# Weights signed by a parametric relu on ScalarE, keys' halves in buffers of their own, and batches prepared in ten timed steps

## The chip, the cores and the metric

One core of one Trainium2 chip. The time is the device time of one execution in microseconds (us), as the median of several runs. The engines are TensorE (PE, matrix products), VectorE (DVE), ScalarE (ACT), GpSimd (POOL) and SyncE (SP), whose queue issues most of the DMA transfers. Each engine works through its own queue in order.

## The reference

```python
k_p = k.reshape(B, H, Sp, 8, D).mean(axis=3)      # B=8, H=8, S=576, D=64, Sp=72
v_p = v.reshape(B, H, Sp, 8, D).mean(axis=3)
scores = q @ k_p.T / 8; scores -= max(scores)
attn = exp(scores); attn /= sum(attn) + 1e-9
x = (attn @ v_p), as 4608 tokens x 512
h = x @ moe_w_in                                  # 512 x 2048
g = where(h >= 1, h, where(h <= -1, 0, (h + 1)**2 / 4))
x = g @ moe_w_out                                 # 2048 x 512
h = x @ moe2_w_in; g = h / (1 + exp(-h))          # the same sizes
out = g @ moe2_w_out
```

## The kernel before

**Numbers.** The products run in float16. Each operand is scaled by a power of two and kept as two halves, hi and lo, and each product is three: hi by hi, hi by lo, lo by hi. The four weights arrive as float64, read as pairs of 32-bit words. A piece of weights (128 x 1024 values, `raw`, or a tile that is lent as a room for it) is turned into halves in this chain: ACT takes the absolute value of the high words, scaled down (`Abs`, L185 or L247); DVE takes their maximum with an accumulator (L190 or L248); PE and DVE spread that maximum over the partitions (L107, L108) and a power of two follows from it in two tiny steps (`w_scale`); DVE shifts the float's bits (L93), ORs the sign bit in from the high word (L202 or L267) and the rest of the mantissa from the low word (L208 or L270); ACT scales (L215 or L273) and casts to hi (L220 or L275); POOL subtracts to get lo (L221 or L276). `moe_w_in` comes in nine pieces, `moe_w_out` in four quarters of two pieces. The second MLP's weights are loaded twice, first only for their maximum (L111), then for the conversion.

**First MLP.** Nine tiles of 512 tokens. For a tile there are 16 steps; each makes one chunk of 128 hidden units in 12 products of 128x512 (tile `hps`, weights `wa`), and the chunk three steps older goes into the output `y` with 12 products (weights `wb`). Between the two, ACT (L823, L830, L862) and DVE (L93, L834, L863) work out the piecewise activation `g`. In the first tile the weights are still being converted, and its `y` products stand behind all its `hps` products, quarter by quarter of `moe_w_out`. The second MLP starts at about 960 us and is 18 half-tiles.

**Attention.** It is worked out ahead of the first MLP, a query tile of 128 rows in four slots: `att_qT` (mean of absolute values on ACT, L465; hi and lo on ACT and DVE, L367 and L368; a DMA transpose from SP, L554), `att_scores` (PE, L564), `att_norm`, then a transpose of the attention weights (`aT`, from SP, L622) and the product with the values (`att_pv`, PE, L657). In the first eight steps of the second tile there are two slots to a step, later one.

**Batches.** Each of the eight batches needs its pooled keys and values. Half of the raw rows are loaded by SP (`kv_load`), the other half added by POOL's accumulating DMA (`kv_more`), DVE adds what is left (L459, L462), ACT takes the mean (L465), PE and DVE turn it into a scale, ACT and DVE split hi and lo, ACT copies both (L499), and SP issues two DMA transposes into `kT` (L502). All this for a batch is called at the first slot of the first query tile that needs it (`batches`). The keys' hi and lo are two tiles `rows`, from the same pool of two buffers as each query tile's own `rows`: the mean of the next query tile (L465) writes into a buffer from which a key transpose reads.

**Order.** A scheduler, led by an estimate of times, puts the instructions of each engine in order; `tc.issue_after` holds single ones behind others. On the chip each engine keeps that order.

Of the kernel before, what the change touches and what calls it, by code (L numbers as in the profile page):

```python
# [28 lines left out]
FLOOR_DOWN = _bits((1023 - 60 - 8 * 112) << 20)  # L29
# [3 lines left out]
def tile_pooled_attention_two_mlps(  # L33
# [79 lines left out]
    cols, free = const.tile([128, 80], F32, name="cols"), iter(range(80))  # L113
# [60 lines left out]
    def steps(piece, dst, scale, loaded, mx=None, seen=None, fill=None):  # L174

        t = {}

        def s0():
            r = t["r"] = piece()
            x = xfp.tile([128, XF], F32, tag="xf", name="xf")
            t["x"] = x[:, 0:r.shape[1] * r.shape[2] // 2].rearrange("p (a b) -> p a b", a=r.shape[1])
            nc.scalar.activation(out=t["x"], in_=high(r, F32), func=AF.Abs, scale=DOWN)  # L185

        def s1():
            x, m = t["x"], mx()
            with after_lows():
                nc.vector.tensor_scalar(  # L190
                    out=x, in0=x, scalar1=0.0, scalar2=FLOOR_DOWN, op0=ALU.max, op1=ALU.max, accum_out=m
                )
            seen()

        def s2():
            xi = t["x"].bitcast(I32)
            with after_lows():
                ts(xi, xi, 3, op0=ALU.logical_shift_left)

        def s3():  # L200
            xi = t["x"].bitcast(I32)
# [4 lines left out]
        def s4():  # L206
            xi = t["x"].bitcast(I32)
            lows.append(nc.vector.scalar_tensor_tensor(  # L208
                out=xi, in0=low(t["r"]), scalar=29, in1=xi, op0=ALU.logical_shift_right, op1=ALU.bitwise_or
            ))  # L210
            loaded()

        def s5():
            x, s = t["x"], scale()
            nc.scalar.activation(out=x, in_=x, func=AF.Copy, scale=s)  # L215
# [9 lines left out]
        return [s0] + [s1] * bool(mx) + [s2, s3, s4, s5]  # L225

    def new_scale(e, g):
        s = sm.tile([128, 1], F32, tag="ws", name="ws", bufs=3)
        w_scale(e, s, g)
        return s  # L230

    def weight_in(w, e, tiles, cuts, rooms):
# [4 lines left out]
        mx, s, g = col(n), col(n), col(n)  # L237
# [4 lines left out]
        def room32(p):  # L242
            return tiles[p].rearrange("p a c f -> p (a c f)").bitcast(F32).rearrange("p (a b) -> p a b", a=KD)

        def look(p):
            x = room32(p)
            nc.scalar.activation(out=x, in_=high(held[p], F32), func=AF.Abs, scale=DOWN)  # L247
            nc.vector.tensor_scalar(  # L248
                out=x, in0=x, scalar1=0.0, scalar2=FLOOR_DOWN, op0=ALU.max, op1=ALU.max, accum_out=mx[:, p:p + 1]
            )  # L250

        def scales(a, b):
# [6 lines left out]
            w_scale(e[:, a:b], s[:, a:b], g[:, a:b])  # L259

        def work(p):
# [3 lines left out]
            xi = x.bitcast(I32)  # L265
            ts(xi, room32(p).bitcast(I32), 3, op0=ALU.logical_shift_left)
            nc.vector.scalar_tensor_tensor(  # L267
                out=xi, in0=high(r, I32), scalar=-0x80000000, in1=xi, op0=ALU.bitwise_and, op1=ALU.bitwise_or
            )
            nc.vector.scalar_tensor_tensor(  # L270
                out=xi, in0=low(r), scalar=29, in1=xi, op0=ALU.logical_shift_right, op1=ALU.bitwise_or
            )
# [1048 lines left out]
```

## Time and profile before

| what | value |
|---|---|
| time, median of 3 runs | 1641.39 us (1640.28 to 1647.74) |
| the profiled execution: time, span | 1640.59 us, 1638.8 us |
| mean granted clock of TensorE | 0.969 of 2.4 GHz |
| busy PE | 1534.5 us (94%) |
| busy DVE | 1208.5 us (74%) |
| busy ACT | 894.1 us (55%) |
| busy POOL | 581.8 us (36%) |

The span is the part of the execution that the profiler records; about 1.8 us lie around it. The first tile of the first MLP ends at 209 us with its output `y`, the second at 333 us, and from there most tiles take 86 to 98 us. PE is busy nearly throughout from 440 us on; the idle time lies before that. The rows below are cited by group.

### The profile page before, as it was taken

The numbers are of one execution on the slowest core, as the hardware profiler recorded it, in microseconds if no ns is written. First come the engines' busy times: TensorE is split into PE (matmuls) and PEld (weight loads), VectorE is DVE, ScalarE is ACT, GpSimd is POOL, SyncE is SP. The second block draws the span as 40 slices with busy tenths as digits, with TensorE's granted clock in tenths as the row PEclk, the third lists the DMA queues.
The fourth block names the chain that finished last, engine by engine and source line by source line (L and its number), as shares of the span: only waits on it lengthen the run. The fifth ranks groups of instructions, "written<-read, shape, count | busy, mean of one in ns | idle before, by whom it ended". The sixth has DMA issues, their size and how long they took to land.

```text
span 1638.8 us, 34439 instructions
## 1 busy us (share of the span) xinstructions
PE 1534.5 (94%) x14278; PEld 1052.6 (64%) x14278; DVE 1208.5 (74%) x2166; ACT 894.1 (55%) x1418; POOL 581.8 (36%) x507
## 2 busy tenths in 40 slices
PE   6765889799999999999999999999999999999998
PEld 5322434344444444444444479999999999999998
DVE  6898868566777687787767767777776777777765
ACT  4477455455666556574566555554444544455543
POOL 2342513113343332331355424433333433343322
PEclk9876899899999999999999999999999999999999
DMA  9573688927547366255574330001100000000000
GB/s 295 123 181 86 122 165 190 186 73 130 145 107 166 89 111 138 81 140 163 194 302 145 148 129 28 27 27 32 36 27 28 27 34 34 27 27 28 27 15 27
DMA packets 226157, 166.35 MB, mean 102 GB/s; under 512 B 154960, under 2 KB 193616, under 8 KB 226000
## 3 DMA queue, kind: packets, MB, share of 16 engines
q1 hardware_dynamic: 216592, 155.88, 35.4%
q0 software_dynamic: 9408, 8.27, 3.7%
q8 instruction: 112, 1.84, 0.5%
q14 instruction: 45, 0.37, 0.1%
HBM read 102.76 MB, written 33.55 MB: 83 GB/s over the span
## 4 chain that ended last, share of the span: by engine, by line
PE 50%; DVE 16%; DMA 9%; issue 9%; ACT 9%; POOL 6%; SPq 1%; DVEq 0%; POOLq 0%; ACTq 0%
PE y L120 5%; PE y L122 5%; PE y L121 5%; PE hps L120 4%; PE hps L122 4%; PE hps L121 4%; PE y L1024 4%; PE y L1025 4%; PE y L1026 4%; PE hb L122 4%; PE hb L121 4%; PE hb L120 4%; POOL c L724 4%; DMA kT<-rows 3%; DMA yin<-y 2%
## 5 line engine op out<-in xcount | busy, mean ns | idle before, releaser
L121 PE MATMUL hb<-xl,wc 128*128 128x128 f16 x2016 | 347.6, 219 | 0.0
L122 PE MATMUL hb<-xh,wc 128*128 128x128 f16 x2016 | 347.6, 219 | 0.0
L120 PE MATMUL hb<-xh,wc 128*128 128x128 f16 x2016 | 347.6, 219 | 0.0
L368 DVE SCALAR_TENSOR_TENSOR g<-c,tsg,g 128x512 f16<-128x512 f32 x252 | 228.7, 910 | 97.8 <-ACT g L367 97.8
L1024 PE MATMUL y<-wd,g 128*128 128x256 f16 x1008 | 274.7, 273 | 1.9 <-DVE ob L1037 1.8
L1026 PE MATMUL y<-wd,g 128*128 128x256 f16 x1008 | 274.7, 273 | 0.0
L1025 PE MATMUL y<-wd,g 128*128 128x256 f16 x1008 | 274.7, 273 | 0.0
L120 PE MATMUL hps<-xh,wa 128*128 128x512 f16 x576 | 222.7, 387 | 36.2 <-ACT wa L275 19.7
L964 ACT ACTIVATE c<-c,tc 128x512 f32<-128x512 f32 x144 | 103.2, 717 | 230.8 <-DVE c L961 230.8
L367 ACT ACTIVATE g<-c,tsg 128x512 f16<-128x512 f32 x252 | 177.6, 718 | 85.8 <-POOL c L727 48.3
L122 PE MATMUL hps<-xh,wa 128*128 128x512 f16 x576 | 220.7, 384 | 3.8 <-POOL wa L276 3.8
L121 PE MATMUL hps<-xl,wa 128*128 128x512 f16 x576 | 222.8, 387 | 0.4 <-DVE xl L368 0.2
L120 PE MATMUL y<-g,wb 128*128 128x512 f16 x544 | 210.0, 388 | 11.6 <-ACT wb L220 9.8
L122 PE MATMUL y<-g,wb 128*128 128x512 f16 x544 | 210.6, 387 | 4.7 <-POOL wb L221 4.7
L121 PE MATMUL y<-g,wb 128*128 128x512 f16 x544 | 210.7, 387 | 0.5 <-DVE g L863 0.5
L121 PEld LDWEIGHTS <-wc 128*128 128x128 f16 x2016 | 197.3, 98 | 2.4
L120 PEld LDWEIGHTS <-wc 128*128 128x128 f16 x2016 | 197.3, 98 | 2.2
L122 PEld LDWEIGHTS <-wc 128*128 128x128 f16 x2016 | 197.3, 98 | 0.0
L961 DVE TENSOR_TENSOR c<-c,hb 128x512 f32<-128x512 f32 x252 | 167.8, 681 | 38.6 <-PE hb L122 36.2
L834 DVE SCALAR_TENSOR_TENSOR g<-g,tbr,u 128x512 f32<-128x512 f32 x144 | 126.4, 878 | 59.0 <-ACT u L830 58.1
L724 POOL TENSOR_TENSOR c<-c 128x512 f32<-128x512 f32 x108 | 164.0, 1533 | 2.8
L603 POOL TENSOR_TENSOR e<-e,den 128x576 f32<-128x576 f32 x36 | 49.6, 1378 | 313.6 <-DVE den L602 226.2
(185 smaller groups left out, 2710.3 us busy)
## 6 DMA issues: line engine op xcount, KB each, us to landing
raw<-in_moe_w_out_dram SPq DMA_DIRECT2D x21, 1024.0 KB
raw<-in_moe_w_in_dram SPq DMA_DIRECT2D x18, 1024.0 KB
y<-y SPq DMA_DIRECT2D x36, 256.0 KB
yin<-y SPq DMA_DIRECT2D x18, 512.0 KB
out_dram<-ob SPq DMA_DIRECT2D x36, 256.0 KB
d<-hl SPq DMA_DIRECT2D x32, 256.0 KB
qt<-in_q_dram SPq DMA_DIRECT2D x31, 256.0 KB
wc<-d SPq DMA_DIRECT2D x8, 896.0 KB
```

What stands on the lines that cost most here:

```text
L120: nc.tensor.matmul(out=acc, lhsT=wh, rhs=xh, start=start, stop=False)
L121: nc.tensor.matmul(out=acc, lhsT=wh, rhs=xl, start=False, stop=False)
L122: anchor["pe"] = nc.tensor.matmul(out=acc, lhsT=wl, rhs=xh, start=False, stop=stop)
L367: a = nc.scalar.activation(out=hi, in_=x, func=AF.Copy, scale=s)
L368: return a, nc.vector.scalar_tensor_tensor(out=lo, in0=x, scalar=s, in1=hi, op0=ALU.mult, op1=ALU.subtract)
L724: nc.gpsimd.tensor_tensor(out=out, in0=a, in1=b, op=ALU.subtract)
L834: anchor["dve"] = nc.vector.scalar_tensor_tensor(out=g32_t[s], in0=g32_t[s], scalar=r["br"], in1=u_t.pop(s), op0=ALU.subtract, op1=ALU.max)
L961: nc.vector.tensor_tensor(out=out, in0=x, in1=y, op=ALU.add)
L964: nc.scalar.activation(out=x, in_=x, func=AF.Silu, scale=r["c1"])
L1024: nc.tensor.matmul(out=acc, lhsT=xh, rhs=wh, start=start, stop=False)
L1025: nc.tensor.matmul(out=acc, lhsT=xh, rhs=wl, start=False, stop=False)
L1026: nc.tensor.matmul(out=acc, lhsT=xl, rhs=wh, start=False, stop=stop)
```

## The change

1. The sign and the magnitude of a weight come from one ACT instruction, a parametric relu with a scale, a bias just under zero and a large negative slope (`signed`); DVE's sign OR is gone. The maximum is taken by DVE from the raw high words (`abs_max`, L113), so the scale is needed before the ACT instruction and not behind the low words. `w_scale` has six tiny steps instead of two.
2. The keys' halves have a tag of their own, `krows`, with two buffers.
3. From batch 2 on, a batch is prepared in ten steps, each at a fixed number of slots ahead of the first slot of its first query tile (`PREP`), and each held behind what was last issued on five engines. Sums have two buffers instead of three.
4. The six steps of the first quarter of `moe_w_out` are spread over steps 6 to 13 of the first tile instead of all at step 10, and the small scale tiles of a query or token tile are columns of one tile (`small`).

```diff
-    def w_scale(e, s, g, up=14):
-        ts(e.bitcast(I32), g.bitcast(I32), 0x7FF00000, 3, ALU.bitwise_and, ALU.logical_shift_left)
-        bits(s, e, -1.0, 254 + up)
+    def w_scale(e, d, s, g, up=14):
+        t = sm.tile([128, 8], F32, tag="wt", name="wt", bufs=2)
+        a, b = (t[:, 4 * i:4 * i + g.shape[1]] for i in range(2))
+        ts(a, g, FLOOR_HIGH, DOWN, ALU.max, ALU.mult)
+        ts(b.bitcast(I32), a.bitcast(I32), EXP_MASK, op0=ALU.bitwise_and)
+        bits(d, b, -1.0, 15 + TOP)
+        ts(b.bitcast(I32), a.bitcast(I32), 0x00700000, 3, ALU.bitwise_and, ALU.logical_shift_left)
+        bits(s, b, -1.0, 254 - 8 * TOP + up)
+        ts(e.bitcast(I32), a.bitcast(I32), 0x7FF00000, 3, ALU.bitwise_and, ALU.logical_shift_left)
+    def signed(x, r, d):
+        nc.scalar.activation(out=x, in_=high(r, F32), func=AF.Prelu, scale=d, bias=under, alpha=-LIFT)
...
     def steps(piece, dst, scale, loaded, fill=None):
         def s0():
-            nc.scalar.activation(out=t["x"], in_=high(r, F32), func=AF.Abs, scale=DOWN)
+            signed(t["x"], r, scale()[0])
         def s1():
-            x, m = t["x"], mx()
-            with after_lows():
-                nc.vector.tensor_scalar(
-                    out=x, in0=x, scalar1=0.0, scalar2=FLOOR_DOWN, op0=ALU.max, op1=ALU.max, accum_out=m
-                )
-            seen()
+            with after_lows():
+                shifted(t["x"])
         def s2():
+            lows.append(with_low(t["x"], t["r"]))
+            loaded()
         def s3():
-            nc.vector.scalar_tensor_tensor(
-                out=xi, in0=high(t["r"], I32), scalar=-0x80000000, in1=xi, op0=ALU.bitwise_and, op1=ALU.bitwise_or
-            )
...
     def weight_in(w, e, tiles, cuts, rooms):
         def look(p):
-            x = room32(p)
-            nc.scalar.activation(out=x, in_=high(held[p], F32), func=AF.Abs, scale=DOWN)
-            nc.vector.tensor_scalar(
-                out=x, in0=x, scalar1=0.0, scalar2=FLOOR_DOWN, op0=ALU.max, op1=ALU.max, accum_out=mx[:, p:p + 1]
-            )
+            abs_max(mx[:, p:p + 1], high(held[p], F32))
...
     def weight_out(w, e, dst, tiles):
+        def look(i):
+            abs_max(mx[d][:, half:half + 1], high(held[i], F32))
+        def search(d):
+            s[d] = new_scale(e[:, d:d + 1], all_of(m[:, 0:1]))
...
-            st[2 * d][:-1] + st[2 * d + 1][:-1] + [st[2 * d][-1], st[2 * d + 1][-1]] for d in range(KD)
+            [lambda d=d: look(2 * d), lambda d=d: look(2 * d + 1), lambda d=d: search(d), st[2 * d][:-1],
+             st[2 * d + 1][:-1], [st[2 * d][-1], st[2 * d + 1][-1]]] for d in range(KD)
...
+    def keys_mean(b):
+        krows[b] = [ap.tile([SPT, H, 2, D], F16, tag="krows", name="krows", bufs=2) for _ in range(2)]
+        sums_mean(sums[b, "k"], km, krows[b][0])
     def batch_keys(b):
-        x = sums.pop((b, "k"))
-        hi, lo = rows(SPT), rows(SPT)
-        s = sums_scale(x, km, ek[:, b:b + 1], hi)
-        split(hi[:, :, 0], lo[:, :, 0], x, s)
+        hi, lo = krows[b]
+        split(hi[:, :, 0], lo[:, :, 0], sums.pop((b, "k")), search(SPT, km, ek[:, b:b + 1]))
...
-    def batches(i):
-        b = segs(i)[-1][2]
-        if i > NI and segs(i - 1)[-1][2] != b:
-            pool_to(8 * b + 4)
-            batch_keys(b)
-            pool_to(8 * b + 8)
-            batch_values(b)
...
+    def due(b):
+        return 4 * (S * b // 128 - 2 * NI) - 3
+    PREP = [
+        (16, lambda b: kv_load(b, "k")), (15, lambda b: kv_load(b, "v")),
+        (13, lambda b: kv_more(b, "k")), (12, lambda b: kv_more(b, "v")),
+        (7, lambda b: sums_of(b, "k")), (6, lambda b: sums_of(b, "v")),
+        (5, lambda b: keys_mean(b)), (4, lambda b: values_mean(b)),
+        (3, lambda b: batch_keys(b)), (2, lambda b: batch_values(b)),
+    ]
+    def prepare(n):
+        for b in range(2, B):
+            for before, f in PREP:
+                if due(b) - before == n:
+                    with behind("pe", "act", "dve", "pool", "sp"):
+                        f(b)
...
+    W2S = [6,7,9,10,11,13]
...
-        if s == 10:
-            run(*work2[0])
+        if s in W2S:
+            with behind("dve", "act", "pe"):
+                w2step(0, W2S.index(s))
```

Three places in the engines' order follow. In the names, `xf` is a piece of weights in work, `wm` a maximum, `u`, `g` and `stash` belong to the activation, `sum`, `rows`, `krows` and `skv` to the keys and values.

DVE before, in the first tile, at the first two pieces of `moe_w_out`:

```order
L190 TENSOR_SCALAR xf,wm_879<-xf 128x1024
L462 TENSOR_TENSOR sum<-raw 72x512
L93 TENSOR_SCALAR u<-g_726,tlim 128x512
L863 TENSOR_TENSOR g_730<-g_693,g_730 128x512
L93 TENSOR_SCALAR xf<-xf 128x1024
L93 TENSOR_SCALAR u<-g_755,tlim 128x512
L202 SCALAR_TENSOR_TENSOR xf<-raw,xf 128x1024
L93 TENSOR_SCALAR xf<-wa_136 128x1024
L368 SCALAR_TENSOR_TENSOR rows<-sum,skv,rows 80x8x64
L834 SCALAR_TENSOR_TENSOR g_726<-g_726,tbr,u 128x512
L208 SCALAR_TENSOR_TENSOR xf<-raw,xf 128x1024
L190 TENSOR_SCALAR xf,wm_879<-xf 128x1024
```

DVE after, at the same two pieces:

```order
L95 TENSOR_SCALAR xf<-xf 128x1024
L191 SCALAR_TENSOR_TENSOR xf<-raw,xf 128x1024
L95 TENSOR_SCALAR xf<-xf 128x1024
L350 SCALAR_TENSOR_TENSOR v_115<-sum,skv,v_115 72x512
L191 SCALAR_TENSOR_TENSOR xf<-raw,xf 128x1024
L95 TENSOR_SCALAR xf<-xf 128x1024
L95 TENSOR_SCALAR u<-g_996,small 128x512
L859 TENSOR_TENSOR stash<-g_944,stash 128x512
L830 SCALAR_TENSOR_TENSOR g_969<-g_969,small,u 128x512
L191 SCALAR_TENSOR_TENSOR xf<-wb_128,xf 128x1024
L113 TENSOR_REDUCE wm_1126<-raw 128x1
```

The row of the sign (L202) has gone from between shift and low words. In the last row a maximum (L113) stands in DVE's queue whose piece is loaded into the buffer that the first low words of this piece of the queue (its second row) have just freed.

ACT before, at batch 3, in the second tile:

```order
L367 ACTIVATE rows<-sum,skv 80x8x64
L367 ACTIVATE v_115<-sum,skv 72x512
L499 COPY rows<-rows 80x8x64
L862 CAST g_2583<-g_2531 128x512
L499 COPY rows<-rows 80x8x64
L823 ACTIVATE g_2579<-hps,tbr,tc_1292 128x512
L830 ACTIVATE u<-u,trsg 128x512
L862 CAST g_2648<-g_2579 128x512
L583 ACTIVATE e<-e,cq 128x576
L465 ACTIVATE rows,eq<-qt 128x512
L823 ACTIVATE g_2644<-hps,tbr,tc_1292 128x512
L465 ACTIVATE rows,eq<-qt 128x512
```

ACT after, at the same batch:

```order
L349 ACTIVATE krows<-sum,skv 80x8x64
L448 ACTIVATE rows,eq<-qt 128x512
L487 COPY krows<-krows 80x8x64
L858 CAST g_2465<-g_2410 128x512
L598 CAST e_116<-e 128x4x72
L598 CAST e_117<-e 128x4x72
L487 COPY krows<-krows 80x8x64
L349 ACTIVATE v_115<-sum,skv 72x512
L819 ACTIVATE g_2461<-hps,small 128x512
L349 ACTIVATE rows<-qt,sq 128x8x64
L349 ACTIVATE xh<-att,small 128x4x128
```

Before, the two copies of the keys are followed by the means of two query tiles into `rows`; now a mean into `rows` stands between split and copies, and the keys are in `krows`.

SP before, at the key transposes of batch 3:

```order
L502 DMA_TRANSPOSE kT<-rows 128x8x80 x2
L147 DMA raw<-in_moe_w_in_dram 128x4x512
L554 DMA_TRANSPOSE qT<-rows 128x8x128
L531 DMA qt<-in_q_dram 128x8x64
L622 DMA_TRANSPOSE aT<-e_116 128x8x128
L622 DMA_TRANSPOSE aT<-e_117 128x8x128
L554 DMA_TRANSPOSE qT<-rows 128x8x128
```

SP after, at the same transposes:

```order
L544 DMA_TRANSPOSE qT<-rows 128x8x128
L149 DMA raw<-in_moe_w_in_dram 128x4x512
L490 DMA_TRANSPOSE kT<-krows 128x8x80
L612 DMA_TRANSPOSE aT<-e_116 128x8x128
L490 DMA_TRANSPOSE kT<-krows 128x8x80
L612 DMA_TRANSPOSE aT<-e_117 128x8x128
L521 DMA qt<-in_q_dram 128x8x64
L544 DMA_TRANSPOSE qT<-rows 128x8x128
```

The key transposes now stand behind a query tile's and among the two of the attention weights, where they stood ahead of all of these.

## Rows read from the trace of the kernel before

**Rows 1.** Busy time by stage, granted clock (PEclk), DMA share.

```profile
47.60:209.00 161.40, 111.04 (x612) 49.63 (x612) 142.36 (x254) 93.98 (x140) 64.43 (x38) 0.81 0.57 126
209.00:312.00 103.00, 84.24 (x536) 39.72 (x536) 71.68 (x174) 53.14 (x97) 24.74 (x24) 0.91 0.92 173
...
916.00:1639.00 723.00, 713.91 (x9296) 656.01 (x9294) 522.10 (x861) 353.42 (x534) 261.68 (x216) 1.00 0.11 39
```

**Rows 2.** The same inside the first tile.

```profile
100.00:150.00 50.00, 26.00 (x120) 10.73 (x119) 48.74 (x89) 34.67 (x55) 14.84 (x8) 0.72 0.65 147
150.00:190.00 40.00, 27.43 (x165) 11.99 (x163) 33.37 (x69) 19.90 (x29) 19.27 (x13) 0.71 0.59 114
```

**Rows 3.** DVE by line, 0 to 210: count, busy, mean ns, idle.

```profile
L248 DVE TENSOR_SCALAR_CACHE_REDUCE wa<-wa 128x1024 f32<-128x1024 f32 (+1 forms) x9 | 9.5, 1096 | 4.2 <-ACT wa L247 4.2
...
L202 DVE SCALAR_TENSOR_TENSOR xf<-raw,xf 128x1024 int32<-128x1024 int32 x5 | 6.9, 1388 | 0.1
...
L267 DVE SCALAR_TENSOR_TENSOR xf<-wb,xf 128x1024 int32<-128x1024 int32 x4 | 4.8, 1212 | 0.0
...
L202 DVE SCALAR_TENSOR_TENSOR xf<-wb,xf 128x1024 int32<-128x1024 int32 x3 | 3.7, 1220 | 0.0
...
L267 DVE SCALAR_TENSOR_TENSOR xf<-room,xf 128x512 int32<-128x512 int32 (+1 forms) x3 | 2.5, 864 | 0.0
...
L267 DVE SCALAR_TENSOR_TENSOR xf<-raw,xf 128x1024 int32<-128x1024 int32 x2 | 2.4, 1217 | 0.0
```

**Rows 4.** DVE's instructions in time (start, us), from two stretches.

```profile
101.36 0.74 DVE L834 SCALAR_TENSOR_TENSOR g<-g,tbr,u 128x512 f32<-128x512 f32 x1
102.02 1.21 DVE L208 SCALAR_TENSOR_TENSOR xf<-raw,xf 128x1024 int32<-128x1024 int32 x1
103.16 1.20 DVE L190 TENSOR_SCALAR_CACHE_REDUCE xf<-xf 128x1024 f32<-128x1024 f32 x1
...
84.86 2.62 DVE L834 SCALAR_TENSOR_TENSOR g<-g,tbr,u 128x512 f32<-128x512 f32 x1
```

**Rows 5.** POOL in time, at 84 us.

```profile
84.70 2.23 POOL L276 TENSOR_TENSOR wa<-xf,wa 128x1024 f16<-128x1024 f32 x1 [6.11 <-ACT wa L275]
```

**Rows 6.** ACT groups, 47 to 209 us.

```profile
L185 ACT ACTIVATE xf<-raw 128x1024 f32<-128x1024 f32 x5 | 5.7, 1137 | 0.6 <-POOL wb L221 0.6
```

**Rows 7.** Loads into tile raw, 40 to 220 us, issue to landing.

```profile
DMA to landing us min/median/max: 6.4/10.1/12.4
```

**Rows 8.** PE's waits, 209 to 440: total, times, longest.

```profile
PE hps L120 <- ACT g L823: 13.9, 4, 6.8
PE att L564 <- DMA qT<-rows: 6.2, 1, 6.2
```

**Rows 9.** PE in time, around 219 us.

```profile
218.46 0.38 PE L121 MATMUL hps<-xl,wa 128*128 128x512 f16 x1
218.68 0.38 PE L122 MATMUL hps<-xh,wa 128*128 128x512 f16 x1
225.82 0.59 PE L120 MATMUL hps<-xh,wa 128*128 128x512 f16 x1 [6.77 <-ACT g L823]
226.20 0.63 PE L121 MATMUL hps<-xl,wa 128*128 128x512 f16 x1
226.63 0.63 PE L122 MATMUL hps<-xh,wa 128*128 128x512 f16 x1
```

**Rows 10.** ACT in time, around 224 us.

```profile
224.38 0.63 ACT L465 ACTIVATE rows<-qt 128x512 f32<-128x512 f32 x1 [8.67 <-DMA kT<-rows]
```

**Rows 11.** ACT in time, 286 to 312 us.

```profile
295.29 0.63 ACT L465 ACTIVATE rows<-qt 128x512 f32<-128x512 f32 x1 [10.21 <-issue]
```

**Rows 12.** Chain that ended last, 205 to 500: start, us, what.

```profile
279.53 20.89 DMA kT<-rows x2
...
304.19 2.76 DMA qT<-rows
...
493.78 9.00 DMA kT<-rows
```

More of the change, by code (lines that the diff above doesn't have):

```diff
@@ L28 @@
 DOWN = 2.0 ** -112
[L29 removed]
+FLOOR_HIGH = _bits((1023 - 60) << 20)
+TOP = 30
+LIFT = 2.0 ** 32
 @with_exitstack
@@ L111, in abs_max @@
         nc.vector.tensor_reduce(out=dst, in_=src, axis=axis, op=ALU.max, apply_absolute_value=True)
-    cols, free = const.tile([128, 80], F32, name="cols"), iter(range(80))
+    cols, free = const.tile([128, 96], F32, name="cols"), iter(range(96))
     def col(n=1):
@@ L264, in work @@
             x = x[:, 0:r.shape[1] * r.shape[2] // 2].rearrange("p (a b) -> p a b", a=KD)
[L265 to L272, printed above, removed]
+            signed(x, r, down[:, p:p + 1])
+            shifted(x)
+            with_low(x, r)
             nc.scalar.activation(out=x, in_=x, func=AF.Copy, scale=s[:, p:p + 1])
@@ L386, in tile_pooled_attention_two_mlps @@
     km, vm = col(), col()
+    under = col()
+    nc.gpsimd.memset(under, -2.0 ** -126)
     ek, ev = col(B), col(B)
@@ L436, in kv_pool @@
         if j == 0:
-            sums[b, which] = kvp.tile([SPT, H, D], F32, tag="sum", name="sum", bufs=3)
+            sums[b, which] = kvp.tile([SPT, H, D], F32, tag="sum", name="sum", bufs=2)
             if which == "k":
@@ L471, in rows, with sums_mean, search @@
         return ap.tile([n, H, 2, D], F16, tag="rows", name="rows", bufs=2)
-    def sums_scale(x, m, e, junk):
-        n = x.shape[0]
+    def sums_mean(x, m, junk):
+        mean(m[0:x.shape[0]], x, junk)
+    def search(n, m, e):
         s = sm.tile([128, 1], F32, tag="skv", name="skv")
-        mean(m[0:n], x, junk)
         all_max(e, m)
@@ L601, in att_norm @@
         )
-        late["dve"] = nc.vector.reciprocal(out=den, in_=den)
+        anchor["dve"] = late["dve"] = nc.vector.reciprocal(out=den, in_=den)
         nc.gpsimd.tensor_tensor(
@@ L786, in small @@
     def small(**names):
-        return {n: sm.tile([128, w], F32, tag="t" + n, name="t" + n, bufs=3) for n, w in names.items()}
+        x = sm.tile([128, sum(names.values())], F32, tag="t" + "".join(names), name="small", bufs=3)
+        r, a = {}, 0
+        for n, w in names.items():
+            r[n], a = x[:, a:a + w], a + w
+        return r
     def consts_A(r):
@@ L1065, in slot @@
             if r == 0 and n < end:
-                batches(n)
                 att_qT(n)
@@ L1074, in att_slots, with sums_of @@
                 if not (n == first and r) and not (n > end and r < 3)]
[L1077 to L1103 removed]
+    done = {"q": 0}
+    def sums_of(b, which):
+        for j in range(4):
+            kv_pool(b, which, j)
+    def due(b):
[13 more added lines that the diff above has]
+                        f(b)
     def q_to(n):
@@ L1195, in tile_pooled_attention_two_mlps @@
         if d + 1 < KD:
-            run(*work2[d + 1])
+            for n in range(6):
+                w2step(d + 1, n)
         for m in range(KF):
```

129 lines of the change are left out of this document (50 added, 79 removed).

## The prediction

> **What bounds the kernel now.** I read first the busy time by stage [rows 1]. From 916 us on PE is busy 713.91 of 723 us at a granted clock of 1.00: the change touches nothing there, and nothing there can be won. The idle time of PE lies ahead of 440 us: 50 of 161.4 us in the first tile (busy 111.04, clock 0.81), 19 of 103 us in the second (84.24, clock 0.91).
>
> In the first tile DVE is the busiest engine, 142.36 of 161.4 us [rows 1]. Taken apart [rows 2], it is full from 100 to 150 us (48.74 of 50) and has some air from 150 to 190 us (33.37 of 40), where PE waits for a chain over four engines rather than for one of them. So an instruction taken from DVE counts whole up to 150 us and in part behind that.
>
> In the second and third tile another thing ends last. PE waits four times, 13.9 us in all, for ACT's L823, once 6.2 us for a query transpose [rows 8]: 20.1 us of idle time. L823 is itself only queued: ACT's mean of a query tile, L465, stands ahead of it and waited 8.67 us for the key transpose to read its buffer `rows` [rows 10], and at batch 3 it stood still for 10.21 us [rows 11], for which the profile names nothing, while the chain names a key transpose of 20.89 us [rows 12]. The chain shows the same transpose at later batches (9.00 us at 493.78 [rows 12]); by then the queues behind have enough ahead of them for PE not to starve. After a wait PE also runs slow: products start 0.22 us apart before the wait and 0.43 us after it [rows 9], which are the levels 2.4 and 1.2 GHz. In the second tile's mean clock of 0.91 that is 0.09 of 84.24 busy us [rows 1], about 8 us. The waits on key transposes thus cost about 20 + 8 = 28 us.
>
> **The change, part by part.** The sum is made against the profiled execution's 1640.59 us.
>
> *Up to 48 us.* The maximum is taken from the raw words by DVE, where it waited for ACT's absolute value, 4.2 us over nine pieces [rows 3]. The scale now has four more tiny steps, in line ahead of the first product. I take -1 us, between -2 and +2.
>
> *First tile, sign.* The sign rows are L202 (5 + 3) and L267 (4 + 3 + 2, two of the room's three at half size): 6.9 + 3.7 + 4.8 + 2.5 + 2.4 = 20.3 us of durations [rows 3]. Such rows overlap a little, 1.14 us from start to start for one of 1.21 us [rows 4], so 15 x 1.14 and two of about 0.6 make 18.3 us of DVE's time. The maximum costs the same as before, an instruction over 1024 columns in the same place of the chain. Four more tiny steps for each of some seven scales, at about 0.07 us from start to start, give back 2 us. All nine of L267 and four of L202, thirteen rows, lie ahead of 150 us, where DVE is full: 13 x 1.14 less 1.4 for five scales, about -13 us. Four lie where it has air: half of 4 x 1.14, about -2. The chain of a piece of `moe_w_out` now has ACT's relu behind the scale instead of ahead of it; the trace shows no relu of this kind, its nearest row is the absolute value of the same shape, 1.14 us [rows 6]. Three later quarters pay that in line, +2 of the 3.4, since the second piece's relu runs beside the first one's shift; a relu of double that cost would add 3 more.
>
> *First tile, looks.* The maxima of reloaded pieces stand in DVE's in-order queue about 5.8, 5.4 and 7.4 us of DVE work (the queue's rows at the durations of their forms) behind the low words that free their buffers (the last row of DVE after shows the first), and a load into `raw` takes 6.4 to 12.4 us, median 10.1 [rows 7]. Before, the waiting instruction was ACT's, and DVE worked on. Behind the waiting maximum stand the activation's `u` and `g`, and the shift of the next piece. At the median the three wait 4.3 + 4.7 + 2.7 = 12 us, at the fastest load 2 us, at the slowest 18.6 us. Part of it falls where DVE has air (150 to 190 us, 6.6 us of it idle) and the wait only moves its idle time: I count 4 us. First tile: -13 - 2 + 2 + 4 = -9 us; from -18 (no look waits, and PE's clock rises with shorter waits) to +4 (all 18.6 us count).
>
> The subtraction on DVE over two inputs took 0.74 us alone and 2.62 us while POOL subtracted [rows 4, 5]; the five sign rows on `raw` were 1.388 us in the mean against 1.22 for the three on `wb`, so signs lost 0.9 us in this way [rows 3], and I count nothing more for it. The Trainium skill (SBUF — State Buffer, Who interferes with whom) says that a DVE instruction with two inputs in SBUF and a GpSimd one that reads SBUF shut each other out for their whole length. By that rule alone, with POOL busy 64 of 161 us and half of a 2.2 us subtraction lost at each meeting, seventeen signs would give back 17 x 0.4 x 1.1 = 7 us; the trace bears out an eighth of that.
>
> *Second and third tile, keys.* With `krows` no query tile's mean waits for a key transpose: the 28 us have no cause any more. What is late next: the scores of the batch's first query tile, which need both `kT`. They are called three slots earlier than before, two steps or more, 11 us at some 5.5 us a step (a tile of 86 to 98 us has 16 steps), so a transpose of 9.00 us lands in time, and one of 20.89 us, as at batch 3, may still be late by a few us [rows 12]. For batch 2 the steps fall into the crowded end of the first tile, and its first use moves ahead of PE's work by some 57 matmuls, so there PE may wait for `kT`: I take 5 us, and another 5 us for the clock and the query transposes that now come ahead of the keys' in SP's queue. -28 + 10 = -18 us, from -28 to -5.
>
> *Behind 435 us.* Waits on the same cause there are small since PE has work queued; -2 us, from -5 to +4 (the fixed order of steps may hold DVE on sums whose loads are late).
>
> Sum: -1 - 9 - 18 - 2 = -30, so 1640.6 - 30 = 1610.6 us; the median of the runs is 0.8 us above the profiled execution, which gives 1611 us.
>
> **The rivals.**
>
> *The looks eat the sign's gain.* DVE waits for each reload, and the first tile stays at its length: 1640.6 - 1 - 18 - 2, about 1620 us. For it speaks that three median loads come to 12 us of waiting, the size of the gain; against it that 6.6 us of DVE's idle time are there to take it.
>
> *The keys' wait only moves.* PE waits for the scores at the new place, or ACT for the sums, and the second and third tile win 5 us: 1640.6 - 1 - 9 - 5 - 2, about 1624 us. For it speaks the landing of 20.89 us, against it the 9.00 us of a later batch [rows 12].
>
> *Neither counts.* The first tile is tied by the latency of its chain, the second by the DMA queues (share 0.92 from 209 to 312 us [rows 1]): -5 in all, 1636 us.
>
> *Slower: key transposes among those of the attention weights.* SP now issues the two `kT` between the two `aT` of a query tile (SP after). If a pair lands as late as 20.89 us [rows 12], the `aT` behind it land later still by some 3 us (the query transpose at 304.19 took 2.76 us [rows 12]), and the next tile's casts into the same attention buffer, three slots or 16 us on (8 us in the double steps), hold ACT as L465 did. That is 24 - 16 = 8 us for four batches and 16 us for two, 64 us of ACT's waiting; PE felt 6.8 of 8.67 us before, so 50 us. Less the 28 and the 12 won, +10, about 1651 us. It decides once a pair takes longer than 13 us; of the two landings shown one does, and that pair went out in the stretch where the DMA queues were fullest, so I give it little.
>
> **How the numbers follow.** Forecast 1611 us: 0.45. Looks eat the gain: 0.18. The wait only moves: 0.17. Neither: 0.10. Slower: 0.10. The range of the forecast itself is 1594 to 1620 us, from about half of each bound; reaching to the two next cases and their spread it is 1594 to 1634 us, which leaves out the slower rival and most of "neither". About 8 us, 0.5%, is what a measurement of this kernel can tell from no change, so faster means below 1633 us: 0.45 + 0.18 + 0.17, 0.80. Same: 0.10, slower: 0.10.
>
> **What would show it.** Right: the first `y` of the first tile leaves at about 199 us instead of 209, and no OR over 1024 columns stands between shift and low words; no ACT row of a query tile's mean waits for a key transpose, and PE's waits between 200 and 435 us come to under 12 us, with a granted clock near 0.97 in the second tile; from 960 us on the same length as before. Wrong: DVE idle ahead of L113 in the first tile, with a load as releaser, for more than 6 us; PE's scores (L564 before) waiting for `kT` at several batches; ACT's casts of the attention weights waiting for `aT`; or a relu row far above 1.14 us.

## The result and the profile after

The changed kernel takes 1621.99 us (median of 4 runs, 1618.14 to 1626.1); the ratio to the kernel before is 0.9898, 95% interval 0.9875 to 0.992. Measured again beside other experiments it came to 0.9904 (0.9889 to 0.9919). The forecast was 1611 us, range 1594 to 1634. So the sign is right, and 11 of the 30 us are missing. The profiled execution took 1618.14 us, span 1616.4.

The stages, as in [rows 1]:

```profile
47.60:209.00 161.40, 106.77 (x618) 48.18 (x617) 130.53 (x272) 108.42 (x159) 57.69 (x38) 0.84 0.65 132
209.00:312.00 103.00, 95.00 (x627) 45.73 (x622) 77.23 (x180) 57.51 (x102) 26.73 (x27) 0.95 0.88 174
916.00:1616.00 700.00, 691.87 (x9196) 645.89 (x9194) 507.15 (x836) 339.12 (x512) 253.33 (x208) 1.00 0.10 34
```

In the first tile DVE's busy time fell by 11.8 us, from 142.36 to 130.53, yet PE got no more work done in the same stretch (618 products in place of 612). From 209 to 312 us PE gained 11 us of busy time and its clock went from 0.91 to 0.95. Where each tile of the first MLP ends shows best in the first output row of each, in the kernel before (first, second and third tile):

```profile
208.99 1.26 ACT L895 ACTIVATE y<-y,cy 128x512 f32<-128x512 f32 x2
...
333.51 0.69 ACT L895 ACTIVATE y<-y,cy 128x512 f32<-128x512 f32 x1 [0.33 <-PE y L122]
...
431.18 0.67 ACT L895 ACTIVATE y<-y,cy 128x512 f32<-128x512 f32 x1
```

and in the changed kernel:

```profile
207.84 1.26 ACT L891 ACTIVATE y<-y,cy 128x512 f32<-128x512 f32 x2 [3.54 <-PE y L124]
...
318.48 0.69 ACT L891 ACTIVATE y<-y,cy 128x512 f32<-128x512 f32 x1 [0.33 <-PE y L124]
...
408.38 0.68 ACT L891 ACTIVATE y<-y,cy 128x512 f32<-128x512 f32 x1
```

The first tile ends 1.2 us earlier, where 9 was forecast; the second takes 110.6 us instead of 124.5, the third 89.9 instead of 97.7, together 21.7 us won, where 18 was forecast. Behind the third nothing changes: 1208.0 us to the end, 1207.6 before.

PE's waits in the first tile, before (us in total, times, longest):

```profile
PE hps L120 <- ACT wa L275: 19.7, 3, 9.4
PE y L120 <- ACT wb L220: 9.8, 3, 5.6
```

and after:

```profile
PE y L122 <- ACT wb L220: 20.8, 2, 16.1
PE att L554 <- DVE sq L97: 8.1, 1, 8.1
PE hps L122 <- ACT wa L263: 7.0, 2, 6.2
```

The waits for converted weights are 27.8 us now and were 29.5: they changed their name from `wa` to `wb` and stayed. The spreading of the maxima (`all`, L109) waited 4.1 and 3.4 us for DVE, where it had waited 2.3 us in all. And new is one wait of 8.1 us of the scores, which leads to a place not forecast. The chain of waits around it:

```profile
151.35 8.98 DMA aT<-e
...
163.84 12.04 DMA qT<-rows
175.97 0.73 ACT rows L448 x2
```

and ACT there, the row behind that transpose:

```profile
175.97 0.63 ACT L448 ACTIVATE rows<-qt 128x512 f32<-128x512 f32 x1 [4.47 <-DMA qT<-rows]
...
176.60 0.45 ACT L349 ACTIVATE xh<-att,small 128x256 f16<-128x256 f32 x1
```

A query tile's transpose took 12.04 us. ACT's next mean, which writes into the buffer that this transpose reads, waited 4.47 us for it, and with it the `xh` behind it in ACT's queue. `xh`, and DVE's `xl` right behind it (177.09 us), read the PSUM buffer `att` that PE's scores needed next (the wait is put down to `sq`, DVE's row after `xl`):

```profile
169.10 0.38 PE L124 MATMUL y<-stash,wb 128*128 128x512 f16 x1
177.63 0.66 PE L554 MATMUL att<-kT,qT 128*128 128x72 f16 x8 [8.15 <-DVE sq L97]
```

PE stood for 8.15 us. It is the picture of [rows 10], with a query's transpose in the place of the keys', and in the first tile instead of the second. Beside this transpose runs the second of POOL's adding loads of batch 2 (`kv_more`):

```profile
164.37 2.11 POOL L414 DMA_DIRECT2D raw<-in_v_dram  x2 [1.80 <-DMA raw<-in_v_dram]
```

From 209 to 440 us PE's waits fell from 22.7 to 8.0 us in all. ACT's waits for transposes went only in part, before:

```profile
ACT rows L465 <- DMA kT<-rows: 23.3, 4, 9.1
ACT rows L465 <- issue: 10.2, 1, 10.2
ACT rows L465 <- DMA qT<-rows: 3.2, 2, 3.0
```

and after:

```profile
ACT rows L448 <- DMA qT<-rows: 22.1, 6, 6.2
```

No mean waits for a key transpose any more, but the waits for query transposes grew from 3.2 to 22.1 us. None of them is over 6.2 us, and no product of `hps` waits for ACT's activation there any more.

### The profile page after: what moved, and what is told of

Read it like the earlier page. It is cut to its first block, busy times and chain, and to the rows that moved or that the text cites. A ratio compares the mean times of both kernels' runs of the same rounds, so it can differ in the third digit from the quotient of the medians.

```text
span 1616.4 us, 34372 instructions
## 1 busy us (share of the span) xinstructions
PE 1522.0 (94%) x14278; PEld 1050.0 (65%) x14278; DVE 1167.7 (72%) x2154; ACT 898.2 (56%) x1418; POOL 563.5 (35%) x508
## 4 chain that ended last, share of the span: by engine, by line
PE 54%; DVE 9%; issue 9%; ACT 7%; POOL 7%; DMA 6%; SPq 0%; DVEq 0%; POOLq 0%; ACTq 0%
PE y L122 6%; PE y L124 5%; PE y L123 5%; PE hps L123 5%; PE hps L124 5%; PE hps L122 5%; POOL c L716 4%; PE y L1020 3%; PE y L1022 3%; PE y L1021 3%; PE hb L122 3%; PE hb L124 3%; PE hb L123 3%; DMA yin<-y 3%; DVE g L350 2%
## 5 line engine op out<-in xcount | busy, mean ns | idle before, releaser
L350 DVE SCALAR_TENSOR_TENSOR g<-c,small,g 128x512 f16<-128x512 f32 x252 | 228.7, 910 | 98.6 <-ACT g L349 98.6
L960 ACT ACTIVATE c<-c,small 128x512 f32<-128x512 f32 x144 | 103.2, 717 | 231.9 <-DVE c L957 231.9
L122 PE MATMUL hps<-xh,wa 128*128 128x512 f16 x576 | 219.7, 382 | 8.5 <-ACT wa L263 7.0
L349 ACT ACTIVATE g<-c,small 128x512 f16<-128x512 f32 x252 | 177.6, 718 | 85.7 <-POOL c L719 48.2
L124 PE MATMUL hps<-xh,wa 128*128 128x512 f16 x576 | 218.7, 382 | 1.6 <-POOL wa L264 1.6
L830 DVE SCALAR_TENSOR_TENSOR g<-g,small,u 128x512 f32<-128x512 f32 x144 | 125.4, 871 | 59.9 <-ACT u L826 58.0
```

Of the source, the lines that this page charges most:

```text
L122: nc.tensor.matmul(out=acc, lhsT=wh, rhs=xh, start=start, stop=False)
L124: anchor["pe"] = nc.tensor.matmul(out=acc, lhsT=wl, rhs=xh, start=False, stop=stop)
L349: a = nc.scalar.activation(out=hi, in_=x, func=AF.Copy, scale=s)
L350: return a, nc.vector.scalar_tensor_tensor(out=lo, in0=x, scalar=s, in1=hi, op0=ALU.mult, op1=ALU.subtract)
L830: anchor["dve"] = nc.vector.scalar_tensor_tensor(out=g32_t[s], in0=g32_t[s], scalar=r["br"], in1=u_t.pop(s), op0=ALU.subtract, op1=ALU.max)
L960: nc.scalar.activation(out=x, in_=x, func=AF.Silu, scale=r["c1"])
```

## The experiments

Ratios are to the kernel before, with a 95% interval. "First y" is the start of the first tile's first output row; as the profiles differ by up to 8 us in when the first wait of PE for weights ends (59.5 to 67.8 us), the length of the first tile is also given from there, and split at the first output product, where PE first uses a quarter of `moe_w_out` (before: 144.2 us, 65.8 up to that product and 78.4 behind it).

| run | ratio (interval) | time, us | first y | first tile from its first wait's end (up to the first output product + behind it) | second, third tile |
|---|---|---|---|---|---|
| the change | 0.9898 (0.9875 to 0.992) | 1621.99 | 207.8 | 146.9 (60.5 + 86.4) | 110.6, 89.9 |
| e1 weights alone | 0.9943 (0.9925 to 0.9961) | 1631.38 | 207.5 | 141.4 (62.6 + 78.8) | 116.0, 96.9 |
| e2 batches alone | 0.9941 (0.9925 to 0.9957) | 1630.79 | 222.6 | 155.1 (66.5 + 88.6) | 109.0, 94.4 |
| e3 four shared buffers | 0.9844 (0.9811 to 0.9876) | 1616.33 | 209.0 | 142.9 (60.5 + 82.4) | 108.6, 89.9 |
| e4 keys' buffers alone | 1.0006 (0.9992 to 1.002) | 1641.69 | 211.3 | 143.5 (66.2 + 77.3) | 123.1, 95.7 |
| e5 four buffers alone | 1.0002 (0.9982 to 1.0023) | 1639.39 | 207.4 | 142.5 (65.8 + 76.7) | 123.6, 94.3 |
| e6 early steps, shared buffers | 0.991 (0.9877 to 0.9942) | 1623.01 | 210.5 | 144.7 (60.5 + 84.2) | 112.1, 91.1 |
| e7 quarter earlier | 0.9831 (0.9797 to 0.9865) | 1609.56 | 203.3 | 142.9 (53.1 + 89.8) | 111.1, 89.9 |
| e8 quarter at step 10 | 0.9904 (0.9879 to 0.993) | 1623.25 | 215.5 | 149.6 (63.0 + 86.6) | 111.9, 89.9 |
| e9 batch 2's loads moved | 0.9851 (0.9832 to 0.9871) | 1612.12 | 200.6 | 140.1 (60.5 + 79.6) | 108.5, 91.0 |
| e10 e7 and e9 together | 0.9836 (0.9822 to 0.9849) | 1609.93 | 202.0 | 141.0 (53.0 + 88.0) | 108.3, 89.9 |
| e11 keys late | 0.9885 (0.987 to 0.9901) | 1617.47 | 207.0 | 147.4 (60.4 + 87.0) | 106.9, 92.1 |
| e12 the change again | 0.9904 (0.9889 to 0.9919) | 1620.37 | 208.7 | 148.0 (60.5 + 87.5) | 111.8, 89.9 |

**The weights alone (e1).** The change's `w_scale`, `signed`, `steps`, `look`, `search` and `W2S`, with the batch steps left as before, of which this shows one line:

```diff
-    def prepare(n):
+    def batches(i):
```

> The kernel before with the change to the weights alone (parametric relu, maxima from the raw words, the first quarter of moe_w_out spread over steps 6 to 13); keys in the shared rows and batches prepared as before. Theory 1 (the sign's gain in the first tile is real, about 9 us by the first y product of moe_w_out, and the batch steps that the whole change moves into the first tile take it back): the first y leaves at 198 to 202 us instead of 209, time 1629 to 1633 us, ratio 0.993 to 0.996. Theory 2 (the second half of the first tile is tied by the chain of the quarters, and DVE's gain never reaches its end): first y at 206 to 210 us, 1637 to 1641 us, ratio 0.998 to 1.000.

It fell between: the time theory 1 named, but the first y of theory 2. The first tile won under 3 us and the second 8.5. In the first tile PE's longest wait is the same as in the whole change, 16.1 us (total, times, longest):

```profile
PE y L122 <- ACT wb L220: 26.4, 2, 16.1
```

DVE (third figure of busy time) was busy 41.99 us from 100 to 150 us, where it had been busy 48.74 [rows 2]. But the time that it saved lies behind PE's wait and not in it. The wait itself (112.68 to 128.75 us), and the stretch behind it:

```profile
112.68:128.75 16.07, 0.00 (x1) 0.00 (x1) 15.73 (x33) 15.75 (x23) 2.08 (x2) 0.50 0.82 184
128.75:150.00 21.25, 19.55 (x106) 8.06 (x106) 13.58 (x31) 10.30 (x17) 6.75 (x3) 0.86 0.43 114
```

While PE stood, DVE and ACT (fourth figure) were both full: the chain of the first quarter (maximum, scale, relu, shift, low words, scaling, cast) shares these two queues with the activation and the attention. So it is in the whole change, in its wait of 16.11 us:

```profile
105.30:121.41 16.11, 0.00 (x1) 0.01 (x1) 15.86 (x32) 15.85 (x23) 0.00 (x0) 0.50 0.52 145
```

The first output product came 3.2 us sooner than before (62.6 us after the first wait's end, 65.8 before), and the rest of the tile took as long as it had (78.8, 78.4). Why the second tile won without its batch steps being touched was not settled.

**The batches alone (e2).** The change's `krows`, `PREP`, `STEP` and `small`, with the weights left as before, of which this shows one line:

```diff
-            signed(t["x"], r, scale()[0])
+            nc.scalar.activation(out=t["x"], in_=high(r, F32), func=AF.Abs, scale=DOWN)
```

> The change to keys and batches alone (buffers of their own, ten steps, two sums), weights as before. Theory 1: the first tile grows by 5 to 8 us from the batch steps in it, the second and third shrink by about 21 us as in the whole change: 1624 to 1629 us. Theory 2: the first tile keeps its 209 us and the others shrink by 21 us: 1617 to 1621 us, the time of the whole change.

Theory 1's sign and above its size: the first tile is 10.9 us longer, the time just past its upper end. Almost all of that lies behind the first output product, before:

```profile
130.56:208.99 78.43, 59.85 (x400) 27.23 (x401) 62.92 (x126) 41.86 (x66) 32.88 (x21) 0.79 0.51 107
```

and in e2:

```profile
133.99:222.62 88.63, 64.45 (x405) 28.59 (x406) 70.48 (x145) 46.37 (x77) 34.55 (x25) 0.77 0.68 125
```

DVE has 7.6 us more to do in this stretch, and the DMA share (last figure but one) rose. New on ACT: its means wait 15.0 us for query transposes in the first tile, 3.6 us before, 11.4 us more:

```profile
ACT rows L464 <- DMA qT<-rows: 15.0, 5, 5.2
```

The chain of waits there:

```profile
167.38 6.84 DMA aT<-e
174.22 8.17 DMA qT<-rows
```

A transpose for the attention weights takes 6.84 us and one for the queries 8.17 us. So the batch steps do cost the first tile its gain. Whether by DVE's work or by their transfers, this run can't tell, since both grew; e9 below moves the transfers alone.

**Buffers (e4, e5, e6).** The keys' buffers alone, on the kernel before:

```diff
-        hi, lo = rows(SPT), rows(SPT)
+        hi, lo = (ap.tile([SPT, H, 2, D], F16, tag="krows", name="krows", bufs=2) for _ in range(2))
```

> The kernel before with one thing from the change: the keys' halves in two buffers of their own (paid for by two sums instead of three and by the joined small tiles); batches called at their first query tile as before, weights as before. Theory 1: the wait behind the key transposes was the shared buffer, so ACT's waits on them go and the second and third tile win 12 to 20 us, with PE now waiting up to 5 us at each of two batches for the keys' transposes themselves: 1620 to 1629 us. Rival (the early steps do it, the buffers alone only move the wait to the scores): 1634 to 1640 us.

The rival, to the letter. Hardly a mean waits for the keys' transposes any more (0.8 us in all); it waits for the query's, which come behind them, as one row of ACT shows:

```profile
303.81 0.63 ACT L465 ACTIVATE rows<-qt 128x512 f32<-128x512 f32 x1 [12.60 <-DMA qT<-rows]
```

and the chain of waits:

```profile
291.31 12.48 DMA qT<-rows
```

Four buffers shared by both, on the kernel before:

```diff
-        return ap.tile([n, H, 2, D], F16, tag="rows", name="rows", bufs=2)
+        return ap.tile([n, H, 2, D], F16, tag="rows", name="rows", bufs=4)
...
-        hi, lo = rows(SPT), rows(SPT)
+        hi, lo = (ap.tile([SPT, H, 2, D], F16, tag="rows", name="krows", bufs=4) for _ in range(2))
```

> The kernel before with query tiles and keys in one pool of four rows buffers (paid for by two sums and the joined small tiles); batches still prepared at their first query tile, weights as before. The buffers of their own alone gave nothing: ACT's waits went over from the keys' transposes to the query tiles' (36.1 us behind them). Theory 1 (that wait too is for one of two buffers): with four, ACT's waits on both fall under 8 us and the second and third tile win 10 to 16 us, 1624 to 1630 us. Theory 2 (the transposes themselves come too late when a batch is prepared at its first query tile, whatever the buffers): PE waits for the transposed keys and queries instead, 1634 to 1641 us.

Theory 2 again: between 208 and 440 us PE's longest wait is for a transposed query (6.2 us before [rows 8]), and ACT's means wait as long for key transposes as they did with two buffers (23.3 us).

```profile
PE att L564 <- DMA qT<-rows: 9.5, 1, 9.5
...
ACT rows L465 <- DMA kT<-krows: 24.5, 3, 9.6
```

And the whole change with the keys back in the shared two:

```diff
-        krows[b] = [ap.tile([SPT, H, 2, D], F16, tag="krows", name="krows", bufs=2) for _ in range(2)]
+        krows[b] = [ap.tile([SPT, H, 2, D], F16, tag="rows", name="krows", bufs=2) for _ in range(2)]
```

> The whole change, but the keys' halves again in the two rows buffers of the query tiles; the ten early steps stay. Theory 1 (buffers and early steps are both needed): ACT waits on the keys' transposes at each batch as before, 20 us or more in all, and the second and third tile lose 10 to 16 of their 21 us: 1630 to 1637 us. Theory 2 (early steps alone do it, since a key transpose no longer stands in the queue right ahead of query transposes): within 4 us of the whole change, 1617 to 1625 us.

Theory 2: 0.991 against 0.9898 and 0.9904 of the change. So the keys' own buffers, to which the prediction gave the gain, gave nothing that these runs can measure, with the early steps or without.

**Which of the early steps (e11).** Loads and sums early, the other steps late:

```diff
-        (5, lambda b: keys_mean(b)), (4, lambda b: values_mean(b)),
-        (3, lambda b: batch_keys(b)), (2, lambda b: batch_values(b)),
+        (1, lambda b: keys_mean(b)), (1, lambda b: values_mean(b)),
+        (1, lambda b: batch_keys(b)), (1, lambda b: batch_values(b)),
```

> The whole change, but the last four of the ten steps (means, split, copies, key transposes, values) all one slot ahead of the batch's first query tile instead of 5 to 2 slots; loads and sums stay early, the keys' buffers stay their own. Theory K (the key transposes must be away before the first query tile's own transposes come): the second and third tile lose 10 to 17 us again, 1630 to 1638 us. Theory L (early loads and sums, and the fixed order, are what helped): within 4 us of the whole change, 1618 to 1626 us.

Theory L: as fast as the change. So the key transposes need not be away early. What is left is that loads and sums are early, and the fixed order; no run takes these apart.

The rows point at POOL's adding loads. In the kernel before, one goes out right beside the key transposes, and the next batch's plain loads stand 5 to 7 us ahead of them:

```profile
272.60 1.20 SPq L426 DMA_DIRECT2D raw<-in_k_dram  x2
...
274.39 1.17 SPq L426 DMA_DIRECT2D raw<-in_v_dram  x2
...
278.52 2.10 POOL L431 DMA_DIRECT2D raw<-in_k_dram  x2 [7.24 <-DVE g L834]
...
279.53 8.83 SPq L502 DMA_TRANSPOSE kT<-rows  x2
```

The pair of transposes takes 8.83 us to issue on SP and 20.89 us to land [rows 12]. With the keys late but the loads early (e11):

```profile
216.93 2.57 SPq L490 DMA_TRANSPOSE kT<-krows  x2
...
266.39 2.75 SPq L490 DMA_TRANSPOSE kT<-krows  x2
...
374.08 1.19 SPq L410 DMA_DIRECT2D raw<-in_k_dram  x2
...
377.36 0.73 SPq L410 DMA_DIRECT2D raw<-in_v_dram  x1
378.18 3.36 SPq L490 DMA_TRANSPOSE kT<-krows  x2
```

At 378 us the plain loads stand closer ahead of the pair than they did before, and it still takes only 3.36 us to issue. What is missing in e11 is an adding load: none goes out within 10 us of any pair from 100 us on. That the adding loads are the cause is read from these rows; no run moves them alone.

**The loads of batch 2 (e9).** The same collision was suspected in the changed kernel's first tile, where batch 2's loads now are. Only they are moved, the plain ones and the adding ones:

```diff
+        if s in (6, 9):
+            kv_load(2, "k" if s == 6 else "v")
+        if s in (8, 11):
+            with behind("pe", "act", "dve"):
+                kv_more(2, "k" if s == 8 else "v")
...
-                if due(b) - before == n:
+                if due(b) - before == n and (b > 2 or before < 12):
```

> The whole change, with only the four loads of batch 2 moved: issued at steps 6, 8, 9 and 11 of the first tile, where the DMA share is 0.2 to 0.5, instead of at 140 to 165 us, where it is over 1 and a query transpose took 12.0 us. Theory 1 (the DMA queues, crowded by batch 2's loads, hold the transposes that PE's 8.1 us wait hangs on): the share from 150 to 180 us falls under 0.8, that transpose takes under 6 us, PE's wait under 3 us, first y 5 to 8 us earlier, 1613 to 1617 us. Theory 2 (the second half of the first tile is a chain of four query tiles' attention and three quarters' conversion, a shorter transpose only moves who waits): transposes get faster, time within 3 us of the whole change, 1619 to 1625 us.

Theory 1; only PE's remaining wait is above its figure. From 150 to 180 us, by the view of busy time, in the change

```profile
150.00:180.00 30.00, 16.00 (x108) 6.72 (x109) 21.61 (x47) 15.01 (x21) 16.84 (x12) 0.73 1.18 190
```

and with the loads moved

```profile
150.00:180.00 30.00, 22.16 (x160) 10.39 (x161) 25.43 (x59) 18.38 (x27) 18.00 (x12) 0.78 0.72 168
```

the DMA share (last figure but one) falls from 1.18 to 0.72, ACT's waits for query transposes in the first tile from 10.5 to 3.2 us, PE's busy time rises from 16.0 to 22.2 us of 30, and PE's wait for the scores falls from 8.1 to 3.9 us. No row gives the landing of that one transpose. The stretch behind the first output product shrank from 86.4 to 79.6 us (78.4 before) while DVE did the same work in it, in the change

```profile
121.41:207.84 86.43, 62.05 (x404) 27.68 (x406) 59.77 (x143) 48.23 (x74) 38.73 (x26) 0.85 0.71 136
```

and with the loads moved

```profile
121.01:200.62 79.61, 62.43 (x404) 28.29 (x406) 59.65 (x144) 48.58 (x74) 35.84 (x22) 0.84 0.55 129
```

So it is the place of these loads that costs there some 7 us, and not DVE's work. The first tile ends at

```profile
200.62 1.27 ACT L891 ACTIVATE y<-y,cy 128x512 f32<-128x512 f32 x2 [3.59 <-PE y L124]
```

8.4 us ahead of the kernel before; about half of that is the earlier end of this profile's first wait, and by length the tile is 4.1 us shorter. The interval (0.9832 to 0.9871) lies clear of the change measured beside it (e12, 0.9889 to 0.9919).

> The whole change again, on the same chip and beside the same runs of the kernel before as the three others, for a closer ratio: 0.987 to 0.992, and the wait of some 8 us in the first tile for the PSUM buffer behind a query transpose in a second profile too, if it is not one execution's chance.

The second profile shows the same wait, 7.1 us at 171 us, behind a query transpose of 11.84 us: no chance of one execution.

**More buffers for the queries (e3).** In the change, `rows` and `krows` become one tag with four buffers:

```diff
-        return ap.tile([n, H, 2, D], F16, tag="rows", name="rows", bufs=2)
+        return ap.tile([n, H, 2, D], F16, tag="rows", name="rows", bufs=4)
...
-        krows[b] = [ap.tile([SPT, H, 2, D], F16, tag="krows", name="krows", bufs=2) for _ in range(2)]
+        krows[b] = [ap.tile([SPT, H, 2, D], F16, tag="rows", name="krows", bufs=4) for _ in range(2)]
```

> The whole change with one pool of four rows buffers for query tiles and keys together, instead of two and two: the same memory. Theory 1, with the wait named (ACT's mean of a query tile waits for the transpose that still reads one of two buffers: 10.5 us in the first tile, and the PSUM buffers that PE's scores wait for are freed behind it): these waits fall to under 2 us, PE's wait of 8.1 us at 169 us goes, first y at 199 to 203 us, 1610 to 1616 us. Theory 2: ACT's waits go too, but PE then waits for the transposed queries themselves or for moe_w_out; first y at 206 to 209 us, 1616 to 1623 us.

Between the two: 0.9844, its interval just clear of e12's, which was measured beside other runs of the kernel before, and touching that of the change's first measurement. ACT waits no more for a query's transpose, and PE's wait behind it is 3.2 us; the transposes stay slow (DMA share 0.96 from 150 to 190 us), but less hangs on them. So four buffers won some 0.6% here; in the kernel before they had won nothing (e5).

**The first quarter's chain (e7, e8).** e7 is e3 with

```diff
-    W2S = [6,7,9,10,11,13]
+    W2S = [4,5,7,8,9,11]
```

> The whole change with four shared rows buffers, and the six steps of moe_w_out's first quarter two steps earlier (4, 5, 7, 8, 9, 11 instead of 6, 7, 9, 10, 11, 13). Theory A (the first tile is tied by the first quarter's chain: PE waited 16 us for its cast while the chain's twelve hops of 7.5 us own work took 22 us in the queues): that wait falls by 6 to 10 us and the first y leaves 6 to 10 us earlier, 1606 to 1612 us. Theory B (DVE's work is what ties it there, full from 100 to 120 us; the order only moves who waits): the wait goes to the last piece of moe_w_in instead, and the time stays at 1613 to 1620 us.

PE's wait for the first quarter fell from 16.6 to 12.2 us, but the tile from its first wait's end is as long as in e3, 142.9 us: the first output product came 7.4 us earlier and the rest of the tile took 7.4 us more. Theory B, in what the profile shows (DVE was busy 11.59 and ACT 12.24 of the 12.24 us of PE's wait); the time, 0.9831 against 0.9844, doesn't tell them apart. All six at step 10, on the change:

```diff
-    W2S = [6,7,9,10,11,13]
+    W2S = [10]
...
-                w2step(0, W2S.index(s))
+                for n in range(6):
+                    w2step(0, n)
```

> The whole change with all six steps of moe_w_out's first quarter at step 10, as before the change, instead of spread over steps 6 to 13. Theory A: the chain starts later, PE's wait for the first quarter grows by 3 to 8 us, 1624 to 1630 us. Theory B: no difference beyond 3 us, 1619 to 1625 us.

Theory B too: no difference in time, though the first output product came 2.5 us later.

**Together (e10).** e7 and e9 in one kernel.

> Four shared rows buffers, moe_w_out's first quarter two steps earlier, and batch 2's loads at steps 6, 8, 9 and 11: what looked best, together. Theory 1: the gains add up, 1602 to 1608 us. Theory 2: no better than without the moved loads, 1607 to 1613 us.

Theory 2: 0.9836, no better than either within the intervals. The gain of e9 is not there: the stretch behind the first output product is 88.0 us. e7, e9 and e10 all beat both kernels: the one before by 25 to 29 us, the change by some 8 to 12.

## Why the prediction was right, and where it was not

*Up to 48 us*, -1: not to be told apart from the 8 us by which the profiles differ there.

*First tile, sign.* DVE's busy time fell by 11.8 us between 47.6 and 209 us, and by 13.5 in e1, where no batch step was moved, against the -16 worked out for the rows. The Trainium skill's rule on two-input DVE instructions beside GpSimd (SBUF — State Buffer, Who interferes with whom) would have added, by the prediction's estimate, 7 us to that; the trace shows none of it.

The term was too large all the same: -13 ahead of 150 us, of which 5.3 us show at the first output product (3.2 in e1) and 2.8 at the end of e1's tile. In part it is the sum: 13 x 1.14 takes two rows of half size for whole ones; with 11 x 1.14 + 2 x 0.6, less the same 1.4, it is -12.3. In the main it is the step "an instruction taken from DVE counts whole up to 150 us". Up to the first output product DVE's work fell from 63.0 to 56.4 us (e1: 58.2), and PE followed it for the larger part; DVE was nearly full there (93%), and in PE's wait ACT was too. Behind that product, from 121 us on, PE did not follow DVE: in e1 DVE had 8.3 us less to do there (54.6 us, 62.9 before) and the stretch was as long as before.

*First tile, looks.* Two of the three waits were there, 6.1 us in all, against 12 at the median load and 4 counted. The prediction had named more than 6 us of them as a sign that it is wrong; with batch 2's loads moved (e9) they were 1.9 us. DVE's group in the change (count, busy, mean ns, idle before):

```profile
L113 DVE TENSOR_REDUCE wm<-raw 128x1 f32<-128x1024 f32 x5 | 6.1, 1213 | 6.1 <-DMA raw<-in_moe_w_out_dram 6.1
```

The relu took 1.32 us, not the 1.14 of the absolute value, well under the bound (ACT's group, same columns):

```profile
L183 ACT ACTIVATE xf<-raw,cols,ws 128x1024 f32<-128x1024 f32 x5 | 6.5, 1324 | 0.0
```

*First tile as a whole*, -9: it came to -1, and by its length from the first wait's end to +2.7 us. The term that the sum did not have is batch 2's loads: moved into the first tile, they were given no price there. A query transpose of some 3 us took 12 beside them, and PE waited 8 us behind it; the stretch behind the first output product grew by 8.0 us (10.2 with the batch steps alone, e2), and with the loads elsewhere (e9) 6.8 of the 8.0 are gone. That e9's first `y` leaves 8.4 us earlier than before looks like the 9 that were forecast, but by length it is 4.1. The rival "the looks eat the sign's gain" had the time, 1620 us, and for the larger part the wrong eater.

*Second and third tile, keys.* -18 forecast, -21.7 measured. The place was right and the size came out, which is partly luck, for the cause named was not the one. "With `krows` no query tile's mean waits for a key transpose: the 28 us have no cause any more" came true in its first half and was worth nothing: with the buffers alone (e4) ACT waits for query transposes instead, with four (e5) as long for the keys', and with the keys back in the shared two the change is as fast (e6). The buffer was where the wait showed; the reader, a transpose that lands late, was what made it long. The ten steps keep it from the next batch's adding loads, and e11 shows that early loads, sums and order do it without early transposes. That it is the adding loads is likely by the rows and not shown by a run. Nor is it shown why PE now stands for none of the 22.1 us that ACT's means still wait, and why the weights alone (e1) won 9.3 us in these tiles, beside 18.8 for the batches alone (e2).

*The time.* 1622 us lies in the range to 1634, but outside the forecast's own 1594 to 1620: only the reach over the next two rivals holds it. That own range is narrower than the working gives: the bounds add to -53 and +5, and half of the way to each is about 1600 to 1629 us. Of the signs named as right, the length behind 960 us and PE's waits from 200 to 435 us (8.0, under 12) came; the first `y` at 199 us did not, and the clock of the second tile rose to 0.95 instead of 0.97.

*The wait only moves* was right for the buffers (e4: nothing, 1.0006). For the whole change it was right for ACT in part (22.1 us for queries) and wrong for PE. *Slower*: the casts and products that wait for `aT` were seen, 5.4 us in one place, far from the 50 us priced.

*Behind 435 us*, -2: +0.4 measured.

## What to carry to other kernels

When a profile names a buffer as what an engine waits for, ask why its reader is late before giving it another buffer: in the kernel before, more buffers won nothing (e4, e5). In the changed kernel moving the loads that ran beside the reader won about half a per cent (e9 against e12), and four buffers about as much (e3), since less hung on each slow transpose. A load that is moved ahead needs a price at the place where it goes, among the transfers that it will stand beside. And look for an engine's air in the stretch in which the engine that bounds the kernel waits: the mean from 100 to 150 us showed 8 us of air on DVE (e1), and in PE's wait of 16 us there was next to none.

## What the runs showed of the hardware

DMA transposes were slow beside POOL's adding loads. The chains of waits, followed back from 210, 320 and 440 us in each of the fourteen traces to 120 us, name 57 landings of transposes. The 20 that took up to 3.6 us all ran with no adding load in flight; the 16 that took 9 us and more all ran beside one, among them the 12.04 us of the change, 11.84 in its second profile, and the 20.89 of the kernel before. Between lie landings of both kinds (without an adding load up to 8.43 us). A high DMA share alone does not do it; in the change, with no adding load in flight (a landing by the chain, and the busy time of that stretch, the DMA share last but one):

```profile
247.62 3.19 DMA qT<-rows
247.62:250.81 3.19, 3.19 (x36) 1.67 (x35) 1.61 (x4) 1.44 (x2) 0.00 (x0) 1.00 1.00 187
```

On SP a pair took 2.6 to 3.4 us to issue in e11 from 209 to 440 us, and 5.5 to 8.8 us in the kernel before from 209 to 440 us, beside adding loads. This is what goes together in the rows; no run moves the adding loads alone.

The parametric relu with a scale and a bias per partition costs 1.32 us for 128x1024 on ACT, where the absolute value cost 1.14 [rows 6].
